# Three PSUM banks chosen by age, a bank held for l4, and one more step ahead of the slots' sums

## The chip, the cores and the metric

The kernel runs on one core of one Trainium2 chip. The time is the device time of one execution in microseconds (us), median of several. Engines are named as the profile names them: PE (TensorE), DVE (VectorE), ACT (ScalarE), POOL (GpSimd), SP (SyncE, which issues the DMAs).

## The reference, cut

Three layers run one behind the other: attention in chunks of 64 tokens (8 batches, 8 heads, 576 tokens of width 64), a feed-forward layer with squared relu (4608 tokens, 512 to 2048 to 512), and a soft mixture of 8 experts with 4 slots each.

```python
scores = scale * np.matmul(q_c, k_c.transpose(0, 1, 2, 4, 3))     # chunk = 64
attn = exp(scores - max); attn = attn / (sum + 1e-09)
x = np.matmul(attn, v_c)                     # -> (4608, 512)
x = (np.maximum(x @ w_in, 0.0) ** 2) @ w_out
logits = x @ phi                             # 32 slots
d = softmax(logits, axis=0); slot_input = d.T @ x
...                                          # 8 small experts on 4 slots each
c = softmax(logits, axis=1)
return c @ slot_out
```

(The softmaxes and the squared relu are abbreviated here.)

## The kernel before, in words

**Tiling.** The 4608 tokens are 36 tiles of 128. Tiles 0 to 8 go through attention in float32 (`attention32`), tiles 9 to 35 in float16 parts (`attention`; its first three, 9 to 11, lie below `FULL` = 12). The feed-forward layer and the soft mixture run over 13 blocks, of three tiles each but for the first two; a block has 16 steps (f = 0 to 15), one for each 128 columns of the 2048. In a step PE makes twelve matmuls into `hps` (L780), ACT and DVE turn them into float16 parts of g, and g goes to the logits (L866, PSUM tile `L`) and, turned, into G. In blocks 4 to 11 (`BY_DMA`) three of the four quads of G are turned by DMA transposes (L854) and not on PE (L815).

**The slots.** `soft(b)` is a generator that goes with block b's logits, one step of it per step of the main loop: L980 scales them (Ls), PE spreads them into l4 (L990), DVE takes the maximum (L1000, L1001), ACT the exponential `dts` (L1004) and `al` (L1007), DVE keeps the maximum (L1008); then lT on PE (L949) and the shares of the tokens (L959 to L971); then tp (L1018), the weights `dd` (L1031) and, in blocks of `BY_DMA`, their float16 parts (L1036, L1037, L1041); last the sums y of weights and G (L1068: 27 float16 matmuls and 3 float32 ones), added to `acc` by DVE (L1048, or L1052 in other blocks).

**The attention of later tiles** runs beside this. For a tile: maxima of q, k and v (DVE L207), a `reduce` over the partitions on PE (L230, L231; read by DVE L240, L243), a flip (L420, read by DVE L425) and a spread (L429, L430; read by L240, L243) for v, float16 parts of q and k (ACT L446, DVE L451), a DMA transpose of q and k (L472), copies (DVE L476), scores on PE (L487 to L489), the softmax (DVE L493, L496, ACT, DVE L507 to L509, POOL L512, ACT L522, POOL L525), a DMA transpose of p (L528), float16 parts of v (POOL L461, DVE L466), pv on PE (L539 to L541) and the result (ACT L545, DVE L551). In `attention32`, L719 is the last step.

**Three banks.** Reduce, flip, spread, scores, pv, l4, lT, tp and sums all write one of three PSUM banks, got from `misc()`. It goes round the three in turn, skipping the banks held. An operation of an attention tile holds its bank until its readers in the table `gives` have been written into the program. An l4 holds nothing: the third call after it gets its bank if no other is held, and then PE waits for the readers of l4.

**What sets the order.** From the main loop on, the order of PE's instructions is as the loop writes them; for DVE, ACT and POOL this holds from step `ALL_FROM` = 23. In each step the loop writes attention operations that are due (`put_until`, `put`), hps and relu, steps of the soft generators, turns of G and logits. `put` writes an operation when its inputs have been written (`emitted`), when they were written enough steps ago (`behind`), and, for one on PE, when not all three banks are held.

Of the kernel before, what the change touches and what calls it, by code (L numbers as in the profile page):

```python
# [20 lines left out]
P = 128  # L21
# [19 lines left out]
FULL = 12  # L41
# [44 lines left out]
def kernel(  # L86
# [25 lines left out]
    dve, act, pool, pe, sp = nc.vector, nc.scalar, nc.gpsimd, nc.tensor, nc.sync  # L112
# [77 lines left out]
    ps_h = ps1.enter_context(tc.tile_pool(name="ps_h", bufs=2, space=PSUM))  # L190
    ps_m = ps1.enter_context(tc.tile_pool(name="ps_m", bufs=1, space=PSUM))
    bank_of, n_misc, turn, held_banks = {}, [0], [None], {}

    def misc():
        x = bank_of.get(turn[0])
        if x is None:
            while n_misc[0] % 3 in held_banks:
                n_misc[0] += 1
            x = n_misc[0] % 3
            n_misc[0] += 1  # L200
            if turn[0] is not None:
                bank_of[turn[0]] = x
        return ps_m.tile([P, 512], F32, tag=f"misc{x}", name="misc")
# [734 lines left out]
    def late_keep(x, eng):  # L938
        moe_keep(NB - 1, NF - LATE + x, eng)
# [35 lines left out]
    def soft(b):  # L975
        nonlocal cmat
        s0, n = blocks[NB if b == 1 else b]
        L, iv = L_ps.pop(b), iv2_all[:, s0 : s0 + n]
        Ls = big.tile([P, 4, P], F32, tag="Ls", name="Ls")[:, :n]
        dve.tensor_tensor(  # L980
            out=Ls, in0=L[:, : n * P].rearrange("p (j t) -> p j t", j=n),
            in1=iv.unsqueeze(2).to_broadcast([P, n, P]), op=ALU.mult,
        )
        if b == 2:
            second_gT[0] = True
        yield
        if cmat is None:
            cmat = const.tile([P, NT, NS], F32, tag="lg", name="cmat", bufs=1)
        l4 = misc()[:, : n * P]
        pe.matmul(  # L990
            l4, sel4.rearrange("p a s -> p (a s)"), Ls.rearrange("p j t -> p (j t)"),
            start=True, stop=True,
        )
        yield
        rm = sm.tile([P, 1], F32, tag="rm", name="rm", bufs=2)
        nm = sm.tile([P, 1], F32, tag="nm", name="nm", bufs=2)
        al = sm.tile([P, 1], F32, tag="al", name="al", bufs=2)
        rsum = sm.tile([P, 1], F32, tag="rsum", name="rsum", bufs=2)
        dts = big.tile([P, 4, P], F32, tag="dts", name="dts")[:, :n]
        dve.tensor_reduce(out=rm, in_=l4, axis=AX.X, op=ALU.max)  # L1000
        dve.scalar_tensor_tensor(  # L1001
            out=nm, in0=rm, scalar=-1.0, in1=run_n, op0=ALU.mult, op1=ALU.min
        )
        act.activation(  # L1004
            out=dts.rearrange("p j t -> p (j t)"), in_=l4, func=ACTF.Exp, bias=nm, accum_out=rsum
        )
        act.activation(out=al, in_=run_n, func=ACTF.Exp, bias=nm, scale=-1.0)  # L1007
        dve.tensor_copy(run_n, nm)  # L1008
        yield
        new_sum(al, rsum)  # L1010
        cs = slots_exp(s0, n, slots_turn(Ls, n, misc()))
        if b > 2:
            yield
        slots_share(s0, n, cs)
        yield
        tp = misc()[:, : n * NS].rearrange("p (j s) -> p j s", s=NS)
        for j in range(n):
            pe.transpose(tp[:, j], dts[:NS, j], ident[:NS, :NS])  # L1018
        dd = wk.tile([P, 3, NS], F32, tag="dd", name="dd", bufs=1)[:, :n]
        parts = None  # L1020
        if b in BY_DMA:
            top, inv = (sm.tile([P, w], F32, tag=f"iv{w}", name="iv", bufs=2) for w in (1, 3))
            dve.tensor_reduce(out=top, in_=iv, axis=AX.X, op=ALU.max)
            dve.reciprocal(inv[:, :1], top)
            dve.tensor_scalar(inv, iv, inv[:, :1], 8.0, ALU.mult, ALU.mult)
            pool.tensor_scalar(
                out=top, in0=top, scalar1=0.125, scalar2=1.0, op0=ALU.mult, op1=ALU.mult
            )
            act.activation(out=acc, in_=acc, func=ACTF.Copy, scale=al)
            iv = inv  # L1030
        dve.tensor_tensor(  # L1031
            out=dd, in0=tp, in1=iv.unsqueeze(2).to_broadcast([P, n, NS]), op=ALU.mult
        )
        if b in BY_DMA:
            parts = aux_of()[1].rearrange("p (l j s) -> p l j s", l=6, j=3)[:, 3 * (b % 2) : 3 * (b % 2) + 3]
            dve.tensor_scalar_mul(parts[:, 0], dd, 4096.0)  # L1036
            dve.scalar_tensor_tensor(  # L1037
                out=parts[:, 1], in0=dd, scalar=4096.0, in1=parts[:, 0],
                op0=ALU.mult, op1=ALU.subtract,
            )  # L1040
            dve.tensor_scalar_mul(parts[:, 2], parts[:, 0], 2.0 ** -12)  # L1041
        if b > 2:
            yield
        y = misc()
        for j in range(n):
            slot_sums(b, y, dd, j, n, parts)
        if b in BY_DMA:
            dve.scalar_tensor_tensor(  # L1048
                out=acc, in0=y, scalar=top, in1=acc, op0=ALU.mult, op1=ALU.add
            )  # L1050
        else:
            dve.scalar_tensor_tensor(  # L1052
                out=acc, in0=acc, scalar=al, in1=y, op0=ALU.mult, op1=ALU.add
            )
        yield
# [253 lines left out]
    convs = {f: conv(f) for f in range(NF)}  # L1309
    emitted = set()  # L1310

    def emit(task, name, op):
        emitted.add((task, name))
        turn[0] = (task, name)
        op()
        turn[0] = None
        if (task, name) in bank_of:
            held_banks[bank_of[task, name]] = [(task, n) for n in gives[name]]
        for x, users in list(held_banks.items()):
            if all(u in emitted for u in users):  # L1320
                del held_banks[x]


    fa, fb = PARTS
# [218 lines left out]
    for i in range(9, NT):  # L1543
        b, j = tile_block[i]
# [7 lines left out]
    def behind(t, op, d):  # L1552

        eng = tiles[d[0][1]][d[1]].eng if d[0][0] == "t" else ""
        gap = (3 if op.eng == "pe" else 2) if eng == "dma" else op.eng == "pe" and eng != "pe"
        return t - placed.get(d, -99) >= gap

    def put(i, stage, t):
        whole = True
        for n, op in tiles[i].items():  # L1560
            me = ("t", i)
            if op.stage <= stage and (me, n) not in emitted:
                full = len(held_banks) == 3 and op.eng == "pe"
                if not full and all(
                    d in emitted and behind(t, op, d)
                    for d in (d if isinstance(d, tuple) else (me, d) for d in op.deps)
                ):
                    placed[me, n] = t
                    emit(me, n, op)
                else:  # L1570
                    whole = False
        return whole
# [58 lines left out]
    t = min(0, min(slots, default=0))  # L1631
# [2 lines left out]
    )  # L1634
    while t < end or any(x >= t for x in slots):
        if t == ALL_FROM:
            ctx.enter_context(
                tc.manual_schedule(engines={getattr(mybir.EngineType, e) for e in ALL})
            )
        put_rest(t)  # L1640
        put_until(t + 1)
        b, f = steps[t] if 0 <= t < len(steps) else (None, None)
        if b == 2 and f % QF == 0:
            put_rest(t, [("s", NB, x) for x in range(f, f + QF)])
        if b is not None:
            end_step = (b, f) == (NB - 1, NF - 1)
            moe_h(b, f)
            moe_relu(b, f)
            if end_step:
                late_turn(0)  # L1650
                late_keep(0, "dve")
            if by_dma(b, f):
                moe_parts(b, f)
            else:
                moe_square(b, f)
            if (b, f) == (NB - 1, NF - 1):
                give((big, f"xb{b % 2}", 1536))
        if 1 <= t <= len(steps) and by_dma(*steps[t - 1]):
            moe_rest(*steps[t - 1])
        for fn in slots.pop(t, []):  # L1660
            fn()
        if b == NB - 1 and f % 2:
            give((big, f"wi{f // 2}", 1024))
        if 0 <= t - LAG < len(steps):
            b, f = steps[t - LAG]
            if (b, f) < (NB - 1, NF - LATE) and not by_dma(b, f):
                moe_turn(b, f)
                moe_keep(b, f)
            if f % QF == QF - 1 and (b, f) != (NB - 1, NF - 1):
                moe_logits(b, f // QF)  # L1670
            if f == NF - 1:
                if b < NB - 1:
                    run_gen(t + 1, soft(b))
                else:
                    soft_last()
        t += 1
# [212 lines left out]
```

## Time and profile before

| | us |
|---|---|
| runs | 778.18, 781.91, 780.79 |
| median | 780.79 |
| profiled execution, its own time | 780.26 |
| its span | 778.5 |

In the span PE is busy 697.9 us (90%), DVE 515.9 (66%), ACT 468.6 (60%), POOL 199.3 (26%); the mean granted clock of PE is 0.96 of full speed. The hps matmuls alone are 419.1 us. Times of a timeline count from the start of the span. A PE timeline's row gives the start, the duration, the engine, the line, the operation with what it writes and reads, how many instructions were put together, and in brackets the idle time before it and what ended it.

### The profile page before, as it was taken

How to read it: one execution, taken by the hardware profiler on the slowest of the kernel's cores; microseconds unless marked ns; L12 is line 12 of the kernel's file. 1: busy time of each engine (PE TensorE's matmuls, PEld its weight loads, DVE VectorE, ACT ScalarE, POOL GpSimd, SP SyncE). 2: the span in 40 equal slices, each digit the busy share in tenths (PEclk: the TensorE clock that was granted, in tenths of full speed). 3: DMA queues.
4: the chain of work that ended last, by engine and by line, in shares of the span. 5: the costliest groups of instructions: out<-in, count | busy, mean ns of one | idle time of the engine just before them, and what ended most of it. 6: DMA issues, size and time to landing. Idle time of an engine off the chain costs nothing.

```text
span 778.5 us, 16656 instructions
## 1 busy us (share of the span) xinstructions
PE 697.9 (90%) x6419; PEld 434.6 (56%) x6419; DVE 515.9 (66%) x1140; ACT 468.6 (60%) x954; POOL 199.3 (26%) x250
## 2 busy tenths in 40 slices
PE   5788999888499899898998998989989999999973
PEld 4677776654356556455565565555655656553443
DVE  4899995356644788797877987878878761213234
ACT  3688887653446676657576666566766765541133
POOL 3222311112212345344332232222422320002010
PEclk9899999989799999999999999999999999999998
DMA  7897833215605778688686886877678997387989
GB/s 154 216 256 195 216 108 121 56 22 115 136 14 96 123 142 152 119 158 157 104 148 127 146 159 124 157 144 137 123 128 153 233 252 223 93 327 289 392 278 352
DMA packets 305743, 129.35 MB, mean 166 GB/s; under 512 B 276736, under 2 KB 293120, under 8 KB 305664
## 3 DMA queue, kind: packets, MB, share of 16 engines
q1 hardware_dynamic: 305664, 128.29, 69.6%
q8 instruction: 50, 0.82, 0.5%
q14 instruction: 29, 0.24, 0.1%
HBM read 78.71 MB, written 9.44 MB: 113 GB/s over the span
## 4 chain that ended last, share of the span: by engine, by line
PE 64%; DVE 18%; DMA 8%; ACT 4%; issue 3%; SPq 1%; POOL 1%; DVEq 0%; ACTq 0%; POOLq 0%
PE hps L780 37%; PE misc L1068 4%; PE L L866 4%; PE gT L815 3%; DMA qkv<-in_q_dram 2%; DVE qk L451 2%; DVE qk L301 2%; DVE am L207 2%; PE ehps L1720 2%; DMA G<-parts 2%; PE misc L487 1%; DMA qkv<-in_v_dram 1%; DMA unit<-in_moe_w_dram 1%; DMA qkT<-qk 1%; DVE parts L847 1%
## 5 line engine op out<-in xcount | busy, mean ns | idle before, releaser
L780 PE MATMUL hps<-xb,wi 128*128 128x384 f16 (+2 forms) x2400 | 419.1, 327 | 0.0
L780 PEld LDWEIGHTS <-wi 128*128 128x128 f16 x2400 | 226.1, 100 | 150.0 <-issue 32.5
L796 ACT ACTIVATE g<-hps 128x384 f32<-128x384 f32 x144 | 70.5, 489 | 141.1 <-PE hps L780 140.6
L803 ACT ACTIVATE g<-g 128x384 f32<-128x384 f32 (+2 forms) x188 | 96.8, 515 | 5.2
L207 DVE TENSOR_REDUCE am<-qkv 128x1 bf16<-128x512 f32 x90 | 59.0, 678 | 17.9 <-DMA qkv<-in_v_dram 10.5
L847 DVE SCALAR_TENSOR_TENSOR parts<-parts,g 128x384 f16<-128x384 f16 x96 | 60.0, 625 | 6.0 <-ACT g L803 5.5
L525 POOL TENSOR_TENSOR p<-ex,p 128x512 f16<-128x512 f32 x27 | 35.5, 1317 | 89.8 <-ACT p L522 89.8
L461 POOL TENSOR_SCALAR vbd<-qkv,avs 64x512 f16<-64x512 f32 x54 | 47.1, 872 | 39.2 <-DVE vbd L181 19.9
L841 ACT ACTIVATE parts<-g 128x384 f16<-128x384 f32 x96 | 50.2, 523 | 7.9 <-DMA G<-parts 5.1
L248 POOL TENSOR_SCALAR iv_all<-avi 128x1 f32<-128x1 f32 x27 | 16.6, 613 | 139.8 <-DVE avi L243 136.0
L213 ACT ACTIVATE G<-gT 128x384 f32<-128x384 f32 (+1 forms) x96 | 43.4, 453 | 11.8 <-PE gT L815 11.7
L815 PE MATMUL gT<-ident,g 128*128 128x128 f32 x276 | 47.6, 278 | 2.5 <-ACT G L213 2.5
L796 ACT ACTIVATE g<-hps,inv_w 128x384 f32<-128x384 f32 (+2 forms) x56 | 29.8, 533 | 30.1 <-PE hps L780 28.6
L466 DVE SCALAR_TENSOR_TENSOR vbd<-qkv,avs,vbd 64x512 f16<-64x512 f32 x54 | 45.7, 846 | 2.9 <-POOL vbd L461 2.1
L451 DVE SCALAR_TENSOR_TENSOR qk<-qkv,as,qk 128x512 f16<-128x512 f32 x54 | 44.7, 868 | 0.8 <-ACT qk L446 0.8
L815 PEld LDWEIGHTS gT<-ident,g 128*128 128x128 f32 x276 | 35.2, 145 | 12.3 <-issue 3.1
L866 PE MATMUL L<-g,wp 128*32 128x384 f32 x384 | 41.9, 498 | 0.0
L512 POOL TENSOR_TENSOR ex<-ex,rs 128x512 f32<-128x512 f32 x27 | 30.6, 1132 | 40.5 <-DVE rs L509 21.2
L487 PE MATMUL misc<-qkT,qbd 128*128 128x64 f16 x216 | 23.3, 198 | 17.0 <-ACT dts L1004 17.0
L446 ACT ACTIVATE qk<-qkv,as 128x512 f16<-128x512 f32 x54 | 35.7, 708 | 2.5 <-DVE as L240 2.5
L1068 PE MATMUL misc<-G,dd 128*32 128x512 f32 x132 | 33.4, 596 | 1.6 <-DVE dd L1031 1.6
L539 PE MATMUL misc<-pT,vbd 128*128 128x64 f16 x216 | 22.3, 195 | 9.8 <-DMA pT<-p 9.8
(213 smaller groups left out, 1169.8 us busy)
## 6 DMA issues: line engine op xcount, KB each, us to landing
unit<-in_moe_w_dram SPq DMA_DIRECT2D x49, 512.0 KB, 6.0
qkv<-in_q_dram SPq DMA_DIRECT2D x72, 128.0 KB, 3.2
qkv<-in_k_dram SPq DMA_DIRECT2D x72, 128.0 KB, 3.4
qkv<-in_v_dram SPq DMA_DIRECT2D x72, 128.0 KB, 3.4
stage<-in_moe_w_in_dram SPq DMA_DIRECT2D x16, 512.0 KB, 4.8
stage<-in_moe_w_out_dram SPq DMA_DIRECT2D x16, 512.0 KB, 6.2
unit<-in_moe_w_dram SPq DMA_DIRECT2D x27, 256.0 KB, 7.5
out_dram<-o SPq DMA_DIRECT2D x20, 256.0 KB, 3.0
```

Of the source, the lines that this page charges most:

```text
L207: dve.tensor_reduce(out=am, in_=src, axis=AX.X, op=ALU.max, apply_absolute_value=True)
L451: dve.scalar_tensor_tensor(out=qk16[:, 2 * a + 1], in0=flat[:, a], scalar=v["s"][:, a : a + 1], in1=qk16[:, 2 * a], op0=ALU.mult, op1=ALU. ...
L461: pool.tensor_scalar(out=dst[0], in0=vin, scalar1=v["sv"][pr], scalar2=1.0, op0=ALU.mult, op1=ALU.mult,)
L466: dve.scalar_tensor_tensor(out=dst[1], in0=vin, scalar=v["sv"][pr], in1=dst[0], op0=ALU.mult, op1=ALU.subtract,)
L780: pe.matmul(hp, wi[f][:, wl, kt], xb[:, xl, kt], start=(nm == 0), stop=(nm == 3 * KT - 1))
L796: act.activation(out=g, in_=hp, func=ACTF.Relu, scale=sc)
L803: act.activation(out=g, in_=g, func=ACTF.Square)
L815: pe.transpose(gt_ps[b, f][:, j], g[:, j * P : (j + 1) * P], ident)
L841: act.activation(out=part[:, 0], in_=g, func=ACTF.Square, scale=2.0 ** -6)
L847: dve.scalar_tensor_tensor(out=part[:, 1], in0=part[:, 0], scalar=-4096.0, in1=g, op0=ALU.mult, op1=ALU.add)
L866: pe.matmul(L_ps[g0][NS * x : NS * x + NS, :n], wp[:, QF * q + x], g[:, x, :n], start=(q == 0), stop=(q == NQ - 1), tile_position=(0, NS * x),
L1068: pe.matmul(y[NS * g : NS * g + NS], lhs, rhs, start=(j == 0 and x == 0), stop=(j == n - 1 and last), tile_position=(0, NS * g), skip_grou ...
```

## The change

The function `misc` gets a second way to choose a bank: from step `ALL_FROM` on (`by_age`) it takes, of the banks that nobody holds, the one whose last use (taking or letting go) is longest ago. `l4` is held under a name of its own until L1008 has been written (`let_go`). In `soft(b)` of the blocks of `BY_DMA` there is one more `yield` between the parts and the sums. In `put`, tiles below `FULL` (9, 10 and 11 among those that come through it) are no more kept back by held banks or by `behind`; ahead of step 23 `misc` may then hand out a held bank when all three are held.

```diff
--- before.py
+++ after.py
@@ -190,11 +190,23 @@
     ps_h = ps1.enter_context(tc.tile_pool(name="ps_h", bufs=2, space=PSUM))
     ps_m = ps1.enter_context(tc.tile_pool(name="ps_m", bufs=1, space=PSUM))
     bank_of, n_misc, turn, held_banks = {}, [0], [None], {}
-
-    def misc():
+    last_use, by_age = {0: 0, 1: 0, 2: 0}, [False]
+
+    def used(x):
+        n_misc[0] += 1
+        last_use[x] = n_misc[0]
+
+    def misc(keep=None):
         x = bank_of.get(turn[0])
-        if x is None:
-            while n_misc[0] % 3 in held_banks:
+        if x is None and by_age[0]:
+            x = min((y for y in last_use if y not in held_banks), key=last_use.get)
+            used(x)
+            if turn[0] is not None:
+                bank_of[turn[0]] = x
+            if keep is not None:
+                held_banks[x] = [keep]
+        elif x is None:
+            while len(held_banks) < 3 and n_misc[0] % 3 in held_banks:
                 n_misc[0] += 1
             x = n_misc[0] % 3
             n_misc[0] += 1
@@ -986,7 +998,7 @@
         yield
         if cmat is None:
             cmat = const.tile([P, NT, NS], F32, tag="lg", name="cmat", bufs=1)
-        l4 = misc()[:, : n * P]
+        l4 = misc(("soft", b))[:, : n * P]
         pe.matmul(
             l4, sel4.rearrange("p a s -> p (a s)"), Ls.rearrange("p j t -> p (j t)"),
             start=True, stop=True,
@@ -1006,6 +1018,7 @@
         )
         act.activation(out=al, in_=run_n, func=ACTF.Exp, bias=nm, scale=-1.0)
         dve.tensor_copy(run_n, nm)
+        let_go(("soft", b))
         yield
         new_sum(al, rsum)
         cs = slots_exp(s0, n, slots_turn(Ls, n, misc()))
@@ -1039,6 +1052,7 @@
                 op0=ALU.mult, op1=ALU.subtract,
             )
             dve.tensor_scalar_mul(parts[:, 2], parts[:, 0], 2.0 ** -12)
+            yield
         if b > 2:
             yield
         y = misc()
@@ -1309,6 +1323,14 @@
     convs = {f: conv(f) for f in range(NF)}
     emitted = set()
 
+    def let_go(*done):
+        emitted.update(done)
+        for x, users in list(held_banks.items()):
+            if all(u in emitted for u in users):
+                del held_banks[x]
+                if by_age[0]:
+                    used(x)
+
     def emit(task, name, op):
         emitted.add((task, name))
         turn[0] = (task, name)
@@ -1316,9 +1338,7 @@
         turn[0] = None
         if (task, name) in bank_of:
             held_banks[bank_of[task, name]] = [(task, n) for n in gives[name]]
-        for x, users in list(held_banks.items()):
-            if all(u in emitted for u in users):
-                del held_banks[x]
+        let_go()
 
 
     fa, fb = PARTS
@@ -1560,9 +1580,9 @@
         for n, op in tiles[i].items():
             me = ("t", i)
             if op.stage <= stage and (me, n) not in emitted:
-                full = len(held_banks) == 3 and op.eng == "pe"
+                full = len(held_banks) == 3 and op.eng == "pe" and i >= FULL
                 if not full and all(
-                    d in emitted and behind(t, op, d)
+                    d in emitted and (i < FULL or behind(t, op, d))
                     for d in (d if isinstance(d, tuple) else (me, d) for d in op.deps)
                 ):
                     placed[me, n] = t
@@ -1634,6 +1654,7 @@
     )
     while t < end or any(x >= t for x in slots):
         if t == ALL_FROM:
+            by_age[0] = True
             ctx.enter_context(
                 tc.manual_schedule(engines={getattr(mybir.EngineType, e) for e in ALL})
             )
```

No engine gets more or fewer instructions. Lines of the changed kernel are 12 to 21 higher than those of before. Three places show what moves.

PE in a steady block (that of soft(4)), from the last matmul of the group of hps ahead of the sums to the logits behind them; `wi` are columns of the first weights; before:

```order
L780 MATMUL hps<-xb_87,wi_1310 128x384
L1068 LDWEIGHTS aux
L1068 MATMUL misc<-G,aux 32x512
...
L230 LDWEIGHTS ones
L230 MATMUL misc<-am,ones 128x2
L231 LDWEIGHTS ones
L231 MATMUL misc<-four,ones 128x2
L780 LDWEIGHTS wi_1310
...
L866 MATMUL L<-g,wp 32x384 x4
```

and after:

```order
L792 MATMUL hps<-xb_87,wi_1310 128x384
L242 LDWEIGHTS ones
L242 MATMUL misc<-am,ones 128x2
L243 LDWEIGHTS ones
L243 MATMUL misc<-four,ones 128x2
L792 LDWEIGHTS wi_1310
...
L1082 LDWEIGHTS aux
L1082 MATMUL misc<-G,aux 32x512
...
L878 MATMUL L<-g,wp 32x384 x4
```

The reduce and a group of twelve hps moved ahead of the sums.

DVE in the same place, from the parts of the weights (`aux`) to the copies for the next scores (`qbd`); before:

```order
L1041 TENSOR_SCALAR aux<-aux 128x96
L466 SCALAR_TENSOR_TENSOR vbd<-qkv_78,avs,vbd 64x8x64 x2
L847 SCALAR_TENSOR_TENSOR parts<-parts,g 128x384
L1048 SCALAR_TENSOR_TENSOR acc<-misc,iv,acc 128x512
L551 SCALAR_TENSOR_TENSOR xb_87<-misc,xb_87 128x4x128
L207 TENSOR_REDUCE am<-qkv_79 128x1
L240 TENSOR_SCALAR as<-misc 128x2
L243 TENSOR_SCALAR ai<-misc 128x2
L439 SCALAR_TENSOR_TENSOR es<-ai 128x1
L847 SCALAR_TENSOR_TENSOR parts<-parts,g 128x384
L476 COPY qbd<-qkT 64x16x64 x2
```

and after:

```order
L1054 TENSOR_SCALAR aux<-aux 128x96
L478 SCALAR_TENSOR_TENSOR vbd<-qkv_78,avs,vbd 64x8x64 x2
L859 SCALAR_TENSOR_TENSOR parts<-parts,g 128x384
L563 SCALAR_TENSOR_TENSOR xb_87<-misc,xb_87 128x4x128
L219 TENSOR_REDUCE am<-qkv_79 128x1
L252 TENSOR_SCALAR as<-misc 128x2
L255 TENSOR_SCALAR ai<-misc 128x2
L451 SCALAR_TENSOR_TENSOR es<-ai 128x1
L859 SCALAR_TENSOR_TENSOR parts<-parts,g 128x384
L1062 SCALAR_TENSOR_TENSOR acc<-misc,iv,acc 128x512
L488 COPY qbd<-qkT 64x16x64 x2
```

The accumulation moved behind six other instructions and still stands ahead of the copies.

PE where tile 9 comes to pv, between the l4 of soft(2) and the next group of hps; before:

```order
L990 MATMUL misc<-Ls,sel_68 128x384
L815 MATMUL gT<-ident,g 128x128 x3
L420 LDWEIGHTS am
L420 MATMUL misc<-aux,am 1x128
L230 LDWEIGHTS ones
...
L815 MATMUL gT<-ident,g 128x128 x3
L539 LDWEIGHTS vbd
L539 MATMUL misc<-pT,vbd 128x64
```

and after:

```order
L1002 MATMUL misc<-Ls,sel_68 128x384
L827 MATMUL gT<-ident,g 128x128 x3
L551 LDWEIGHTS vbd
L551 MATMUL misc<-pT,vbd 128x64
...
L432 LDWEIGHTS am
L432 MATMUL misc<-aux,am 1x128
L242 LDWEIGHTS ones
```

The pv of tile 9 moved ahead of the flip and reduce, and with that ahead of a group of hps.

## Rows read from the trace of the kernel before

**Rows 1.** Waits of PE over the span: us in total, times, longest.

```profile
PE misc L487 <- ACT dts L1004: 17.0, 7, 3.0
PE misc L539 <- DMA pT<-p: 9.8, 1, 9.8
...
PE misc L1068 <- DVE aux L1036: 5.2, 6, 1.1
...
PE misc L429 <- DVE xb L719: 2.5, 1, 2.5
```

**Rows 2.** Stretches: length, busy us (instructions) by engine, clock, DMA share, GB/s.

```profile
333.80:385.06 51.26, 48.02 (x440) 28.28 (x439) 41.46 (x95) 33.88 (x68) 21.80 (x25) 0.97 0.73 139
...
589.75:633.00 43.25, 43.25 (x402) 26.16 (x400) 35.06 (x84) 30.78 (x62) 13.01 (x15) 1.00 0.92 209
```

**Rows 3.** Timeline of PE around one wait of the scores.

```profile
363.61 2.11 PE L780 MATMUL hps<-xb,wi 128*128 128x384 f16 x12
...
367.96 0.19 PE L487 MATMUL misc<-qkT,qbd 128*128 128x64 f16 x1 [2.10 <-ACT dts L1004]
...
368.68 3.77 PE L780 MATMUL hps<-xb,wi 128*128 128x384 f16 x12
```

**Rows 4.** Timeline of PE: hps behind the first and the last wait.

```profile
267.68 3.08 PE L780 MATMUL hps<-xb,wi 128*128 128x384 f16 x12
...
574.09 3.47 PE L780 MATMUL hps<-xb,wi 128*128 128x384 f16 x12
```

**Rows 5.** Timeline of ACT at the wait of Rows 3.

```profile
367.26 0.56 ACT L1004 ACTIVATE dts<-misc,nm 128x384 f32<-128x384 f32 x1
```

**Rows 6.** Timeline of DVE in the same block.

```profile
364.98 0.16 DVE L240 TENSOR_SCALAR as<-misc 128x2 int32<-128x2 int32 x1
...
368.13 0.15 DVE L1008 COPY run_n<-nm 128x1 f32<-128x1 f32 x1 [1.23 <-ACT al L1007]
...
373.07 0.26 DVE L959 TENSOR_REDUCE cm<-misc 128x3 f32<-128x96 f32 x1 [2.15 <-PE misc L949]
...
374.07 0.16 DVE L240 TENSOR_SCALAR avs<-misc 128x1 int32<-128x1 int32 x1 [0.45 <-PE misc L430]
...
379.06 1.27 DVE L207 TENSOR_REDUCE am<-qkv 128x1 bf16<-128x512 f32 x2
...
387.93 0.85 DVE L476 COPY qbd<-qkT 64x1024 f16<-64x1024 f16 x2
```

**Rows 7.** Timeline of PE: sums, the group behind them, the next scores.

```profile
382.15 0.40 PE L1068 MATMUL misc<-G,aux 128*32 128x512 f16 x3 [1.14 <-DVE aux L1036]
...
384.92 2.11 PE L780 MATMUL hps<-xb,wi 128*128 128x384 f16 x12
...
389.95 0.20 PE L487 MATMUL misc<-qkT,qbd 128*128 128x64 f16 x1
```

**Rows 8.** Timelines of PE and POOL from 184 to 213 us.

```profile
184.70 0.18 PE L429 MATMUL misc<-tm,ones 1*128 1x1 bf16 x1 [2.51 <-DVE xb L719]
...
184.86 3.51 PE L780 MATMUL hps<-xb,wi 128*128 128x384 f16 x12
...
191.69 0.20 PE L487 MATMUL misc<-qkT,qbd 128*128 128x64 f16 x1
...
203.09 1.16 POOL L525 TENSOR_TENSOR p<-ex,p 128x512 f16<-128x512 f32 x1 [3.01 <-ACT p L522]
...
210.90 0.21 PE L539 MATMUL misc<-pT,vbd 128*128 128x64 f16 x1 [9.81 <-DMA pT<-p]
...
212.42 2.89 PE L780 MATMUL hps<-xb,wi 128*128 128x384 f16 x9
```

**Rows 9.** Timeline of PE at two short waits, and the group behind.

```profile
153.06 0.55 PE L815 MATMUL gT<-ident,g 128*128 128x128 f32 x3 [1.80 <-ACT G L213]
154.34 0.90 PE L815 MATMUL gT<-ident,g 128*128 128x128 f32 x3 [0.73 <-ACT G L213]
...
157.27 3.65 PE L780 MATMUL hps<-xb,wi 128*128 128x384 f16 x12
```

## The prediction

> **What bounds the kernel now.** I read the waits of TensorE (PE) first, because the kernel's middle is a row of blocks in which PE has nearly all the time. The list of waits [rows 1] names four that belong to the three "misc" banks or to work that is late: 17.0 us in seven waits of the scores (L487) for the exponential of soft (ACT L1004), 9.8 us in one wait of pv (L539) for a transposed p, 5.2 us in six waits of soft's sums (L1068) for the float16 parts (L1036), 2.5 us in one wait of a spread (L429) for L719. Together 34.5 us. Next I read stretches [rows 2]: a steady block from 333.8 to 385.06 takes 51.26 us, PE busy 48.02, VectorE (DVE) 41.46, granted clock 0.97 on the mean; from 589.75 to 633.00, without soft's waits, PE is busy all 43.25 us at clock 1.00 with DVE at 35.06 (81%). So PE sets the block, and what can be won there is its idle 3.2 us and what the low clock adds.
>
> **A wait costs more than itself.** In one block [rows 3] twelve hps matmuls take 2.11 us at full clock. Then the scores wait 2.10 us and the next twelve take 3.77. All seven such waits are followed by a slow group, the first of 3.08 us, the last of 3.47 [rows 4]; the seven sum to 24.8 us, against 7 x 2.11 = 14.8, so **10.0 us** more.
>
> **Why the scores wait.** Scores of the next tile write the bank that l4 of soft had. Nothing on PE needs l4's readers; the bank does. L1004 starts at 367.26, takes 0.56 [rows 5], and the scores start at 367.96 [rows 3].
>
> **The change part by part.**
>
> *1. The bank by age, l4 held until L1008 is written.* No instruction is added. The scores behind l4 now get the bank of the reduce that stood right ahead of l4's flip (readers DVE L240/L243). These two end at 365.21 in this block (L240 at 364.98 [rows 6], two short rows), before PE comes to the scores at about 365.9. So the wait of 2.10 goes whole, seven times: **-17.0**, and the slow group behind it: **-10.0** (bounds: the clock falls anyway, 0, or all of it). What is late next: lT (L949) gets l4's bank, and must wait for the exponential that ends at 367.82 [rows 5]; without the stall PE is there at 365.9 + 0.7 (scores) + 2.1 (hps) = 368.7. It waits for nothing, with 0.9 in hand.
>
> *2. One more step between the parts and the sums.* Sums (27 float16 and 3 float32 matmuls) go behind the reduce and one more group of hps; the accumulation (DVE L1048) goes behind L551, L207, L240, L243, L439 and L847, ahead of the copy L476. Before, PE is done with hps at 382.15 - 1.14 = 381.0 and waits 1.14 for the sums [rows 7]. With an hps group of 2.11 between, the sums wait only if DVE is more than 2.11 later against PE. **-5.2** in six waits. What pays for it: DVE. PE comes to the reduce about 2.1 + 1.7 + 0.1 = 3.9 us earlier than before, at 377.1 by the clock of the old trace. DVE makes up part of it: its own waits of 2.15 before L959 and 0.45 before L240 go, and 0.44 ahead of L493, 3.04 in sum, while 1.23 for the exponential (L1008) stays [rows 6]. Its two L207 (the reduce's input) then end at 379.06 + 1.27 - 3.04 = 377.3: the reduce waits some 0.2. At the end of the chain the copy L476 (385.74 instead of 388.78) feeds the next scores, which PE wants at 389.95 - 3.9 - 1.1 + 0.2 = 385.2 [rows 7]: 0.5. So a new wait of some 0.7 a block, between 0 and 1.5: **+5** for seven blocks (0 to 10.5). Queued behind the waiting scores are the next hps, and all else on PE. DVE then has 41.46 us of work in a block of about 47.3, 88%, against 81% in the stretch of [rows 2] that ran without a wait.
>
> *3. Tiles 9 to 11 put without the two rules.* Flip, reduce, spread, scores and pv of tile 9 move up. The scores of tile 9, now at 191.69, go ahead of the flip of that stretch, one group of hps and three gT before the spread at 184.70 that waited 2.51: to 184.7 - 2.5 - 2.6 = 179.6, 12 us earlier. The chain behind them (exponential, division, p) follows: POOL's last part of p ends at 203.09 + 1.16 = 204.25 now, and would end at about 192, and its transpose some 3 us later. (Before, the transpose stood behind other transfers, and pv got it only at 210.90.) PE came to pv at 210.90 - 9.81 = 201.1; the new place is one group and three gT earlier, 198.5, less the 3.9 of the spread below, plus new waits of some 1.4: 196, and p is there at 195. So the wait of 9.81 goes: **-9.8** [rows 8]; bounds 0 and 9.8, and I take all, with 1 us in hand. The nine hps behind it took 2.89 where nine of twelve at 2.11 would take 1.58: **-1.3**. The spread that waited 2.51 for L719 is now ahead, and the twelve hps behind it took 3.51, so **-2.5 and -1.4** [rows 8]. New: DVE's L207 of the next tiles now stands ahead of L1052 and waits for loads, which delays the sums and L719 by some 0.6; Tp and the spread of 10 take other banks, 0.8; red of tile 12 takes l4's bank, and waits for the exponential, by the 2.10 of [rows 3] some 1.9; a remainder of 0.7 for scores that stand nearer to their copies. **+4** (1 to 9). Net -11.
>
> *4. The queue of SyncE* gets the transposes of tile 9 ahead of those of 10 and loads of 11 somewhat earlier. Their bytes are the same. In the blocks, the transposes of G have a group of hps less of slack; I cost it at nothing, since PE reads G two steps later; if that cover went, the sums would wait, at most the 1.14 of today a block.
>
> The tail (from 690 on) waits for weights by DMA, asked for by an order that starts when the sums of the last soft are done; it shifts as a whole. 0.
>
> **Sum.** -17.0 - 10.0 - 5.2 + 5 - 11 = -38.2. The profiled execution took 780.26 us (span 778.5), the median of the runs is 780.79, so the sum stands for both: 780.3 - 38.2 = **742**. Own range: the new waits at 0 and 10.5, the early net at -14 and -6: 734 to 753.
>
> **A rule that speaks against it.** In the rows, a wait of 1.14 is followed by hps at full clock (2.11 [rows 7]), one of 2.10 by 3.77; but two short ones, 1.80 and 0.73, 0.5 us of work apart, were followed by 3.65 [rows 9]. The Trainium skill (TensorE: Matmul & The Clock Gate, section "A second HAM failure mode: psum-queue depth-cycling") says that a PE which goes round through PSUM banks pauses so often for a moment that the clock goes up and down, and the throughput is lost in the returns. By that, a bank found by age that leaves short waits would not give the clock back; by the row at 382.15 it would. This is rival B.
>
> **Rivals.**
> A, the forecast: 742.
> B, the short waits keep the clock down: the new 0.5 and 0.2 come near each other, and one group of hps a block runs at 3.77 instead of 2.11 [rows 3]: 7 x 1.66 = 11.6, time **754**. For: [rows 9]. Against: [rows 7].
> C, DVE becomes the bound: from L240 at 374.07 to the two L207 at 379.06 it waits for nothing even now [rows 6], so it has a backlog there that a faster PE does not shorten. If the scores wait 2.0 rather than 0.7, +9, and at such a wait the clock falls [rows 3], +11.6: **763**. For: 88% load. Against: the 81% with no wait at all [rows 2].
> D, the early part gives its gain back (p of tile 9 stays late because its exponential and copies stand behind work of tile 8): **753**.
> E, slower: the reduce now stands ahead of a group of hps and of the sums, so all of PE waits where formerly only the reduce was behind. If the two L207 are kept from their loads, PE waits x in each of eight blocks, plus 1.66 of low clock. The gain of 38 is eaten at 8 (x + 1.66) = 38, x = 3.1 us; at x = 3.8 the time is 780.3 + 5.5 = **786**. For: these loads run on a queue in which transposes take their turn. Against: in the block read, L207 starts at 379.06 with no wait of its own [rows 6].
> F, it does not do what it says: held banks push the same waits onto another user (with one bank held, two are left for six kinds of users): the 17.0 comes back under other names: **779**.
>
> **How the numbers follow.** Chances: A 0.50, B 0.10, C 0.15, D 0.11, E 0.08, F 0.06. A measurement of this kernel can tell about 0.5% (3.9 us) from no change. A to D are faster by more: 0.86. F: same, 0.06. E: slower, 0.08. The range leaves out E and F (0.14) and a little of the ends of A: from 731 (the early net and the new waits at their best, and some slow pieces of scores that I left out) to 765 (C with its end).
>
> **What would show it.** In the changed profile: PE's waits have no entry of L487 on L1004 (step 1); the hps after l4 take 2.1, not 3.8; the sums have no wait on L1036 (step 2), and instead the scores a wait on L476 or the reduce one on L207, below 1.5 a block; blocks last about 47.3; pv has no wait of several us on pT and the hps that now start at 229.91 start near 219 (step 3). Wrong would be: a new wait of over 2 us a block on PE, with a clock below 1.00 behind it (B, C, E), or an unchanged block length (F).

## The result: 743.2 us, and the profile after

The changed kernel's median is 743.16 us (741.49 to 746.41, four runs) against 780.31; the ratio is 0.953, interval 0.949 to 0.957. Its profiled execution took 742.11 us, with a span of 740.3. Beside other kernels on another chip it came to 742.87, ratio 0.955 (0.952 to 0.958). In the changed kernel the scores are L499, soft's exponential is L1016, the sums are L1082, the copies L488, the hps matmuls L792.

The waits of PE over the span (us in total, times, longest), to be set beside [rows 1]:

```profile
PE misc L499 <- DVE qbd L488: 4.2, 6, 1.1
PE misc L1082 <- DVE dd L1044: 3.6, 3, 2.6
...
PE misc L709 <- DVE cmat L972: 3.1, 1, 3.1
...
PE misc L242 <- ACT dts L1016: 1.7, 1, 1.7
...
PE misc L441 <- DVE xb L563: 1.1, 1, 1.1
```

The four entries of [rows 1], 34.5 us, are all gone. In their place are six waits of the scores for their copies, 4.2 us, and a few single ones in the early stretch. Now two steady blocks, as stretches (length, then busy us and instructions of PE, PEld, DVE, ACT, POOL, then clock, DMA share, GB/s):

```profile
314.45:361.68 47.23, 46.16 (x442) 27.73 (x440) 41.41 (x95) 33.46 (x68) 22.01 (x24) 1.00 0.92 155
361.18:408.50 47.32, 46.25 (x440) 27.60 (x439) 40.87 (x95) 33.48 (x68) 16.83 (x18) 1.00 0.82 151
```

The first is the block of [rows 2]: 51.26 us became 47.23. PE is busy for less (46.16 instead of 48.02), since the granted clock is 1.00 instead of 0.97, and its idle time is 1.1 us instead of 3.2. DVE has the same 41.4 us of work.

Where the time went is best seen by following one matmul through both traces. These are starts of the same hps matmul (counted from the first, which is number 0), in us:

| hps matmul number | before | after | difference |
|---|---|---|---|
| 432 | 161.97 | 158.99 | -3.0 |
| 480 | 184.86 | 185.25 | +0.4 |
| 576 (block 3) | 226.88 | 217.98 | -8.9 |
| 720 (block 3) | 261.50 | 252.60 | -8.9 |
| 768 (behind the first scores' wait) | 277.20 | 264.26 | -12.9 |
| 1920 (behind the seventh) | 584.00 | 546.66 | -37.3 |
| the last | 694.95 | 657.04 | -37.9 |

So 8.9 us are won ahead of block 3, 28.4 in seven blocks, and what comes behind is shifted as a whole.

In detail, the block of [rows 3], PE and ACT in the changed kernel:

```profile
347.66 2.11 PE L792 MATMUL hps<-xb,wi 128*128 128x384 f16 x12
...
349.85 0.20 PE L499 MATMUL misc<-qkT,qbd 128*128 128x64 f16 x1
...
350.56 2.11 PE L792 MATMUL hps<-xb,wi 128*128 128x384 f16 x12
352.51 0.75 PE L961 MATMUL misc<-sel,Ls 128*128 128x32 f32 x6
```

```profile
351.31 0.56 ACT L1016 ACTIVATE dts<-misc,nm 128x384 f32<-128x384 f32 x1
```

The scores start at 349.85, directly behind the hps, while the exponential of l4 starts only at 351.31: they no longer have to do with one another. The next twelve hps take 2.11 us (they took 3.77), and lT, which now has l4's bank, starts at 352.51 without a wait.

The place of the sums and the next scores, PE and then DVE:

```profile
361.18 2.11 PE L792 MATMUL hps<-xb,wi 128*128 128x384 f16 x12
363.22 0.40 PE L1082 MATMUL misc<-G,aux 128*32 128x512 f16 x3
...
369.90 0.20 PE L499 MATMUL misc<-qkT,qbd 128*128 128x64 f16 x1 [1.07 <-DVE qbd L488]
...
370.61 2.11 PE L792 MATMUL hps<-xb,wi 128*128 128x384 f16 x12
```

```profile
368.34 0.74 DVE L1062 SCALAR_TENSOR_TENSOR acc<-misc,iv,acc 128x512 f32<-128x512 f32 x1
369.00 0.85 DVE L488 COPY qbd<-qkT 64x1024 f16<-64x1024 f16 x2
```

The sums start without a wait. The next scores wait 1.07 us for the copies, which DVE starts at 369.00, directly behind the accumulation of the sums (0.74 us). The wait is followed by hps at full clock.

### The profile page after: what moved, and what is told of

It reads as the page before. It is cut to its first block, busy times and chain, and to the rows that moved or that the text cites. A ratio compares the mean times of both kernels' runs of the same rounds, so it can differ in the third digit from the quotient of the medians.

```text
span 740.3 us, 16650 instructions
## 1 busy us (share of the span) xinstructions
PE 680.3 (92%) x6419; PEld 426.1 (58%) x6419; DVE 515.6 (70%) x1140; ACT 466.9 (63%) x954; POOL 200.2 (27%) x250
## 4 chain that ended last, share of the span: by engine, by line
PE 52%; DVE 27%; DMA 10%; ACT 4%; issue 4%; SPq 1%; POOL 0%; DVEq 0%; POOLq 0%; ACTq 0%
PE hps L792 30%; DMA qkv<-in_q_dram 3%; PE gT L827 3%; DVE am L219 3%; DVE vbd L478 3%; PE L L878 3%; DVE parts L859 2%; PE misc L1082 2%; DVE qk L463 2%; DVE qk L313 2%; PE ehps L1741 2%; DMA qkT<-qk 1%; DMA qkv<-in_v_dram 1%; DVE qbd L488 1%; DMA unit<-in_moe_w_dram 1%
## 5 line engine op out<-in xcount | busy, mean ns | idle before, releaser
L792 PE MATMUL hps<-xb,wi 128*128 128x384 f16 (+2 forms) x2400 | 406.4, 321 | 0.0
L792 PEld LDWEIGHTS <-wi 128*128 128x128 f16 x2400 | 222.1, 98 | 141.2 <-issue 18.8
L859 DVE SCALAR_TENSOR_TENSOR parts<-parts,g 128x384 f16<-128x384 f16 x96 | 55.9, 582 | 7.3 <-ACT g L815 6.8
L478 DVE SCALAR_TENSOR_TENSOR vbd<-qkv,avs,vbd 64x512 f16<-64x512 f32 x54 | 50.4, 933 | 3.0 <-POOL vbd L473 2.2
L878 PE MATMUL L<-g,wp 128*32 128x384 f32 x384 | 46.1, 496 | 0.0
L1082 PE MATMUL misc<-G,dd 128*32 128x512 f32 x132 | 33.4, 597 | 3.6 <-DVE dd L1044 3.6
L488 DVE COPY qbd<-qkT 64x1024 f16<-64x1024 f16 x54 | 22.8, 422 | 8.3 <-DMA qkT<-qk 8.0
L499 PE MATMUL misc<-qkT,qbd 128*128 128x64 f16 x216 | 22.0, 194 | 4.3 <-DVE qbd L488 4.2
```

What stands on the lines that cost most here:

```text
L478: dve.scalar_tensor_tensor(out=dst[1], in0=vin, scalar=v["sv"][pr], in1=dst[0], op0=ALU.mult, op1=ALU.subtract,)
L792: pe.matmul(hp, wi[f][:, wl, kt], xb[:, xl, kt], start=(nm == 0), stop=(nm == 3 * KT - 1))
L859: dve.scalar_tensor_tensor(out=part[:, 1], in0=part[:, 0], scalar=-4096.0, in1=g, op0=ALU.mult, op1=ALU.add)
L878: pe.matmul(L_ps[g0][NS * x : NS * x + NS, :n], wp[:, QF * q + x], g[:, x, :n], start=(q == 0), stop=(q == NQ - 1), tile_position=(0, NS * x),
L1082: pe.matmul(y[NS * g : NS * g + NS], lhs, rhs, start=(j == 0 and x == 0), stop=(j == n - 1 and last), tile_position=(0, NS * g), skip_grou ...
```

## The experiments

The change has three parts: the banks (by age, with l4 held), the step ahead of the sums, and the two rules of `put`. Each was run alone, and each was taken from the whole.

**The banks alone.** `misc` and the held l4 as in the change; the other two parts as before:

```diff
             dve.tensor_scalar_mul(parts[:, 2], parts[:, 0], 2.0 ** -12)
-            yield
...
-                full = len(held_banks) == 3 and op.eng == "pe" and i >= FULL
+                full = len(held_banks) == 3 and op.eng == "pe"
...
-                    d in emitted and (i < FULL or behind(t, op, d))
+                    d in emitted and behind(t, op, d)
```

> The bank by age and the held l4 alone; the step ahead of the sums and the rules of put are as in before. Theory 1 (the scores wait for the bank alone): PE's wait of the scores on the exponential is gone (17.0 to 0) with the slow clock behind it, 28 us; the sums, with PE 3.9 us earlier and DVE only some 3.0, wait about 2.0 a block instead of 1.1 (+6), and after a wait of 2 us the clock falls once a block (+11 if it does). So 758 if the clock stays up, 770 if it falls; I lean to about 764. Rival (the step is what frees PE, the banks only rename the wait): 778 to 780, with as much wait in all as before.

Measured: 757.94 us, ratio 0.970 (0.964 to 0.976). The waits on the exponential are gone, and the sums wait more than before, as the sum of DVE's and PE's gains had it. Waits of PE, and one of them in the timeline with the group of hps behind it:

```profile
PE misc L1081 <- DVE aux L1049: 9.4, 6, 2.0
```

```profile
421.96 0.40 PE L1081 MATMUL misc<-G,aux 128*32 128x512 f16 x3 [1.62 <-DVE aux L1049]
...
424.73 2.11 PE L792 MATMUL hps<-xb,wi 128*128 128x384 f16 x12
```

9.4 us in six waits, where it was 5.2. The hps behind them are at full clock each time, so the time is that of the case "the clock stays", 758, and the lean to 764 was wrong. The clock did fall once, though: behind the longest wait, 2.04 us, it was the sums themselves that ran slowly. Here is that wait, and then the sums of this block and of the next as stretches, in the columns used above (the clock is 0.62 and then 1.00):

```profile
324.35 0.61 PE L1081 MATMUL misc<-G,aux 128*32 128x512 f16 x3 [2.04 <-DVE aux L1049]
```

```profile
324.35:328.80 4.45, 4.45 (x36) 1.74 (x37) 3.46 (x5) 0.24 (x1) 2.79 (x2) 0.62 0.86 170
373.97:376.74 2.77, 2.77 (x36) 1.30 (x37) 2.71 (x5) 0.50 (x1) 2.19 (x2) 1.00 0.70 147
```

They took 4.45 us instead of 2.77. Behind the other five waits, 1.24 to 1.66 us, the sums took 2.77. So the loss of 1.7 us came once and not in six blocks.

**By age, l4 not held.**

```diff
-        l4 = misc(("soft", b))[:, : n * P]
+        l4 = misc()[:, : n * P]
```

(and the other two parts out, as above)

> The bank by age alone, l4 not held. By the banks as the program gives them out, the flip ahead of the scores gets the bank of l4 now, and the scores that of pv. Theory 1: the same wait of about 2.1 us with the same low clock stands in front of the flip, under the name of ACT's exponential, seven times: 780, at most 3 us off. Rival (the age rule alone frees the scores, holding l4 does little): 750 to 756, and no wait of PE on the exponential.

Measured: 785.94 us, ratio 1.007 (1.004 to 1.010). Its waits of PE:

```profile
PE misc L432 <- ACT dts L1016: 18.2, 7, 3.2
```

The same seven waits stand one instruction earlier, ahead of the flip (L432). The rule by age finds l4's bank to be the oldest when the flip comes; it doesn't know that ACT still reads it. The time missed the expectation (780, at most 3 off): behind the seven came an eighth wait, of the scores for the exponential at 626.01, 2.10 us with a slow group behind it (3.47).

**l4 held, banks in turn.** The hold as in the change, but `by_age` stays off, and the branch that goes round in turn takes the hold:

```diff
...
             x = n_misc[0] % 3
             n_misc[0] += 1
+            if keep is not None and late[0]:
+                held_banks[x] = [keep]
...
-            by_age[0] = True
+            late[0] = True
```

(and the other two parts out, as above)

> l4 held until its maximum is kept, but the banks go round in turn as before. By the program the hold ends ahead of the scores, and the scores of the next tile still get l4's bank. Theory 1: the seven waits of about 2.1 to 3 us stay, 780, at most 3 us off. Rival (holding is what matters): 750 to 756.

Measured: 779.67 us, ratio 0.996 (0.992 to 0.999). Its waits of PE:

```profile
PE misc L501 <- ACT dts L1018: 17.1, 7, 2.8
```

The hold ends when L1008 of before has been written into the program, which is ahead of the scores; then the turn comes to l4's bank and gives it out. Neither half takes the waits away by itself: the hold keeps the flip off the bank, and the age, which counts letting go as a use, keeps the scores off it.

**The step alone.** Only the new `yield`.

> The one more step ahead of the sums alone. Theory 1: six waits of the sums for the parts (5.2 us in all) go, the waits of the scores for the exponential stay (17.0), and nothing new comes, since PE reaches the next scores some 1 us after the copies: 775. Rival (the step only moves the wait from the sums to the copies or to the reduce): 780.

Measured: 767.08 us, ratio 0.981 (0.976 to 0.985): 14 us less, not 5. The sums' wait is gone, and the scores' waits on the exponential are all there (17.5 us in seven). Much of the rest is the clock. Two of the seven waits in its timeline:

```profile
418.36 0.19 PE L499 MATMUL misc<-qkT,qbd 128*128 128x64 f16 x1 [2.43 <-ACT dts L1016]
...
419.06 2.11 PE L792 MATMUL hps<-xb,wi 128*128 128x384 f16 x12
```

```profile
466.82 0.19 PE L499 MATMUL misc<-qkT,qbd 128*128 128x64 f16 x1 [2.43 <-ACT dts L1016]
...
467.52 3.68 PE L792 MATMUL hps<-xb,wi 128*128 128x384 f16 x12
```

The same wait of 2.43 us, with the same scores behind it, is followed once by hps at full clock and once at the low one. Four of the seven brought the clock down here; in the kernel before it was seven of seven (two of them in [rows 4]). The seven groups behind the waits sum to 19.7 us, against 24.8 before, 5.1 less. With the 5.2 of the sums that makes 10.3, and the profiled execution, which was the slowest of the four, has its last hps matmul 10.6 earlier. What the other three won beyond that, no trace shows.

**The whole without one part.** Three kernels, each with one part undone: without `put`'s rules, without the step, without the banks.

> The changed kernel with the two rules of put as before (bank by age with held l4, and the step ahead of the sums, stay). Theory 1: the early stretch loses what the changed trace gained there, 8.9 us at the hps matmul that starts at 217.98 instead of 226.88; PE waits about 10 us for a transposed p again, and the blocks are as in the changed kernel: 752. Rival (the early gain comes from banks by age): 743.

> The changed kernel without the step ahead of the sums (banks by age with held l4, and put, stay). Theory 1: the sums wait about 1.6 us in six blocks, as with the banks alone (9.4 us), in place of the waits for the copies and for the reduce (5.9 us) in the changed kernel, and the clock stays up in nearly all blocks, as it did with the banks alone: 747 to 750. Rival (the step is what keeps the clock up in the changed kernel): a low spell in most blocks, 755 to 762.

> The changed kernel without banks by age and without holding l4 (the step ahead of the sums and the rules of put stay). Theory 1: the seven waits for the exponential are back, 17 us, but as with the step alone the clock falls at only some of them, so the parts add up: the step alone took 14 off the median, put alone 8 to 9: 757. Rival (the fall of the clock depends on where the waits come and is back in all seven): 763 to 766.

And the rules of `put` alone:

> The two rules of put alone (no bank by age, no held l4, no step). Theory 1: the early stretch gains by itself, since there the banks go round in turn in both kernels until step 23: the hps matmul at 226.88 starts some 9 us earlier, and the blocks keep their seven waits: 771. Rival (without banks by age the earlier operations run into other waits for banks): 778 to 782.

All of them by ratio to before, each measured on the same chip as its runs of before, and in us of 780.3:

| parts in the kernel | median, us | ratio (interval) | worth, us |
|---|---|---|---|
| put | 770.03 | 0.990 (0.987 to 0.994) | 7.5 |
| step | 767.08 | 0.981 (0.976 to 0.985) | 15.2 |
| banks | 757.94 | 0.970 (0.964 to 0.976) | 23.5 |
| step, put (without banks) | 760.94 | 0.978 (0.975 to 0.982) | 17.2 |
| banks, put (without step) | 752.26 | 0.967 (0.964 to 0.970) | 25.8 |
| banks, step (without put) | 751.10 | 0.967 (0.964 to 0.971) | 25.7 |
| all | 742.87 | 0.955 (0.952 to 0.958) | 35.3 |

The parts alone sum to 46, the whole is worth 35: the step and the banks win the same thing in part, the clock of the groups behind the scores (5.1 us in the trace of the step alone). How much they share is not settled. The runs come from three chips, an interval is up to 4.5 us to either side, and single traces show less: at the last hps matmul put, step and banks alone are 8.3, 10.6 and 21.6 us earlier than before, 40.5 in sum, and the whole 37.9 and 39.2 in its two traces.

The `put` rules came out as expected, 770.0 alone (771 expected) and 751.1 taken out (752). Without them, the wait of pv is back, which settles what that part does:

```profile
PE misc L551 <- DMA pT<-p: 10.5, 1, 10.5
```

Without the banks the waits on the exponential are back (16.9 us in seven) and again four of them bring the clock down: 760.9 lies between the two expectations. Without the step the sums wait 9.3 us in six, and the time, 752.3, is above the 747 to 750 of theory 1 and below the rival's range; behind one of the six waits, 2.03 us, the sums were slow (4.47 us), and behind the others not. Of `put`'s two rules only one acts. With the distance in steps lifted for tile 9 alone, the program has the same order of instructions on PE and DVE as with both rules lifted for 9 to 11; with only the rule on full banks lifted, it has the order of the kernel without `put`'s part. Neither of these two was run.

**One step more for the accumulation.** The rows at 368.34 and 369.00 suggest moving the accumulation behind the copies:

```diff
             slot_sums(b, y, dd, j, n, parts)
         if b in BY_DMA:
+            yield
             dve.scalar_tensor_tensor(
                 out=acc, in0=y, scalar=top, in1=acc, op0=ALU.mult, op1=ALU.add
```

> The changed kernel with the accumulation of the sums one step later still, behind the copies for the next scores on DVE. Theory 1: in the changed kernel the scores wait 4.2 us in six blocks for these copies, and the accumulation of 0.74 us stands ahead of them; each wait gets shorter by up to that: 4 us less, 739. Rival (another operation is late by as much, the reduce or the spread that gets the bank of the sums): 743.

> The changed kernel with the accumulation one step later still. Its blocks gained 3.4 us on the changed kernel from one hps matmul to the same one seven blocks on, while an early low spell of the clock cost it 2.2. Theory 1: that early spell is not its own, so it is 3 us faster than the changed kernel in the mean of the runs: 740. Rival (what the copies gain, the early stretch always gives back): the same within 1.

> The changed kernel once more, beside the next two on the same chip, so that a difference of half a per cent can be told: 743, blocks of some 47.2 us, the scores' six waits for the copies 4.2 us.

Measured first: 741.41 us, ratio 0.952 (0.949 to 0.956), where 739 was expected; that ratio alone doesn't tell it from the changed kernel. Beside the changed kernel on the same chip: 737.83 us, ratio 0.948 (0.945 to 0.952), against 742.87 and 0.955 (0.952 to 0.958). So it is 5 us faster than the changed kernel, and the fastest of all. The waits of the scores in its trace:

```profile
PE misc L499 <- DVE qbd L488: 0.8, 2, 0.4
```

4.2 us became 0.8. From the hps matmul number 576 to number 1920 its trace gained 32.3 us on before, the changed kernel 28.4.

**Of the distance in steps, only that of the scores lifted**, on top of that kernel (`qk` is the scores; the rule on full banks stays lifted for tiles 9 to 11):

```diff
-                    d in emitted and (i < FULL or behind(t, op, d))
+                    d in emitted and ((i < FULL and n == "qk") or behind(t, op, d))
```

> As the one before, but of the two rules of put only the distance in steps is lifted, and for the scores of tile 9 alone; flip, reduce and spread of tile 9 stay where they were before. Theory 1: the early gain hangs on the scores of tile 9 coming 12 us earlier, with p and its transpose; the 9.8 us wait of pv goes, the spread's 2.5 stays, and the 3.1 of Tp and some of the 2.6 of the sums do not come: 738 to 740. Rival (the whole chain of tile 9 must come earlier): pv waits again some us, 745 to 750.

Measured: 743.26 us, ratio 0.957 (0.953 to 0.960), 5.4 us over the kernel that it was made from. Theory 1 fell; the rival's wait is back, though its time of 745 to 750 was too high. In its timeline:

```profile
203.19 0.21 PE L551 MATMUL misc<-pT,vbd 128*128 128x64 f16 x1 [6.20 <-DMA pT<-p]
...
204.83 3.08 PE L792 MATMUL hps<-xb,wi 128*128 128x384 f16 x12
```

The pv came up with the scores by a group of hps, but p did not come early enough, since the scores had moved by one group only: they still stood behind the spread of tile 9. With the whole chain of the tile moved, as in the changed kernel, pv does not wait.

## Why the prediction was right, step by step

**1. The banks.** Forecast -27.0 for seven waits and the slow groups behind them. At the seven places the hps matmuls gained 4.0, 3.9, 3.8, 4.2, 3.8, 3.8 and 4.7 us, 28.2 in sum. The readers of the new bank had ended, as read from [rows 6], and lT had its slack. Rival F came closer to being true than its 0.06 says: with either half of the bank rule it is what happens, 786 and 780 us. Its own time was added up wrongly: with the 17.0 and the 10.0 back, 742 becomes 769, and 779 would need the early gain gone as well.

**2. The step ahead of the sums.** Forecast -5.2 and +5, a net of nothing. In the changed kernel the sums don't wait, the copies cost 4.2 and the reduce's maxima 0.3; between the seven places the traces differ by 0.2 us in all (28.4 less 28.2). The arithmetic that gave it, DVE makes up 3.0 of PE's 3.9, is borne out by the kernel with the banks alone, where the sums' waits grew from 5.2 to 9.4, 0.7 each. But "a net of nothing" is not what the step is worth. By the medians it costs some 9 us to take it from the whole. From matmul 576 to the last, the traces with and without it differ by 6.9: without it the sums wait 9.3, in place of 4.5 for the copies and the maxima, and lose 1.7 to the clock once. The rest lies ahead of matmul 576, where low spells move from run to run. My sum was right since it took the parts in one order; the -5.2 is no price of the step. In the expectation for the step alone I took it for one, and missed by 8 us, of which 5.1 in the trace are the clock.

**3. Tiles 9 to 11.** Forecast -11 (-14 to -6), measured -8.9, with some luck. The hps forecast near 219 (229.91 before) starts at 221.0. The chain came as worked out: the last part of p ends at 192.6 (192 forecast), pv starts at 196.64 without a wait (196 forecast).

```profile
191.42 1.16 POOL L537 TENSOR_TENSOR p<-ex,p 128x512 f16<-128x512 f32 x1 [0.74 <-ACT p L534]
...
196.64 0.19 PE L551 MATMUL misc<-pT,vbd 128*128 128x64 f16 x1
```

The term that was mis-sized is the new waits, +4. From matmul 432 to 576, PE idles 10.6 us, where it was 15.8. The old waits of 9.8 and 2.5 are gone, so 7.1 are new. In the timeline of PE:

```profile
171.21 1.09 PE L709 MATMUL misc<-ident,ex 128*128 128x128 f32 x4 [3.11 <-DVE cmat L972]
172.09 4.05 PE L792 MATMUL hps<-xb,wi 128*128 128x384 f16 x12
...
199.36 0.16 PE L242 MATMUL misc<-am,ones 128*128 128x2 bf16 x1 [1.71 <-ACT dts L1016]
...
211.91 2.78 PE L1082 MATMUL misc<-G,dd 128*32 128x512 f32 x24 [2.62 <-DVE dd L1044]
```

The reduce of tile 12 waits 1.71 on l4's bank (1.9 forecast). But Tp, a transpose in the attention of tile 8 (L709), waits 3.11, which is 2.5 more than before, and the spread of tile 10 waits 1.1 (0.8 forecast for the two); the hps behind Tp run at the low clock, 4.05 instead of 2.11. The sums wait 2.62, which is 1.7 more than before (0.6 forecast). Against this, the low clock behind [rows 9] is gone in this run, 3.0 us by the first line of the table, which the forecast did not have. That is luck and not the change: the kernels with the banks alone and with l4 held alone, whose `put` is that of before, gained 2.6 us there too. From matmul 432 to 576 alone, step 3 gained 5.9 us, just short of its range (6.1 in the second trace). The low spells of this stretch move from run to run of the same kernel: in the second trace of the changed kernel, the hps behind Tp took 2.11, and matmul 576 was 9.75 earlier, not 8.9.

**4. The queue and the tail** cost nothing, as forecast: from matmul 1920 to the last the difference grows by 0.6.

**The rivals.** B, after the rule of the Trainium skill (TensorE: Matmul & The Clock Gate, "A second HAM failure mode: psum-queue depth-cycling"), did not come about: the changed kernel's PE still goes through three banks, waits some 0.7 us six times, and no group of hps in the blocks is slow. Without the banks, four of seven waits of 2.1 to 2.7 us brought the clock down. So of waits at the same place, the six of up to 1.1 us were harmless and the longer ones not always. C did not come either; DVE is at 88% of the block (41.41 of 47.23), and late by what the forecast said. Of D, 753, and E, 786, nothing shows: the early gain stayed, and the reduce waits for its maxima in one block, 0.3 us.

## What to carry to other kernels

When one engine waits for another through a shared buffer, look who still reads what the buffer held before, not only who makes the data; a rule that spreads buffers by age needs to know when the last reader is done, or it hands the same wait to the next in line. A part of a change has no price of its own where two parts remove the same loss: take it out of the whole and put it in alone, and quote both. And in a queue worked in order, an accumulation that nobody waits for belongs behind the copy that somebody does.

## What the runs showed of the hardware

The seven waits of the scores for the exponential, 2.1 to 3.0 us, stand in five of these kernels. In the kernel before, with l4 held alone and with the rules of `put` alone, the hps behind all seven were slow, 21 of 21. In the two with the step (alone, and with `put`) it was four of seven each, with rows that differ in nothing else that I can see ([2.43] followed by 2.11 and [2.43] followed by 3.68). In the first three the sums also wait, 0.7 to 1.2 us in six blocks; with the step they don't. Each of the two differs from a kernel with seven falls by the step alone. So, by one trace of each, the step itself took part of the falls away. How it does so is not shown.

Ahead of the sums, waits of 1.24 to 1.78 us were harmless in the kernels without the step that have the new banks, ten of ten, and the two of 2.03 and 2.04 were followed by sums at a mean clock of 0.62. But a wait of 2.62 ahead of 24 float32 sums, early in the changed kernel, was followed by full clock. So a fall may not be added to a wait's price as a fixed term. Its size in the five kernels was 0.7 to 1.7 us for twelve hps; whether it comes is not settled by the length of the wait alone, and what decides it stayed open.
